# Blockwise attention and a tanh-shrink layer on one core: transposes one by one inside the units, small weight sums moved into two products, other accumulation banks

## The chip, the cores and the metric

One core of one Trainium2 chip runs the kernel. The metric is device time in microseconds (us) for one execution; lower is better. All work is in 32-bit floating point.

## The reference

`lam` decays the attention; the result is laid out token by token and goes through a dense layer, `h - tanh(h)`, and a second dense layer.

```python
# q, k, v: (4, 8, 768, 64); w_in: (512, 2048); w_out: (2048, 512)
for b in range(S // 64):
    qb, kb, vb = (t[:, :, 64*b : 64*b + 64] for t in (q, k, v))
    intra = einsum('bhic,bhjc->bhij', qb, kb) * Dmask          # lam**(i-j), i >= j
    out[:, :, sl] = einsum('bhij,bhjd->bhid', intra, vb) + einsum('bhid,bhde->bhie', qb * lam_pow, kv_state)
    kv_state = lam_block * kv_state + einsum('bhsd,bhse->bhde', kb * rev_pow, vb)
x = out.transpose(0, 2, 1, 3).reshape(3072, 512)
h = x @ w_in
result = (h - tanh(h)) @ w_out
```

## The kernel before

**Tiling.** The 3072 tokens are worked off in six groups (`g` = 0 to 5) of 512: 128 positions of each of the four batch entries, which the kernel calls blocks 0 to 3. Blocks 0 and 1 are the pair `P0`, 2 and 3 the pair `P1`. While the dense layers of group `g` run, the attention of group `h = g + 1` is slipped between them in small pieces: the function `pieces(g, place)` (L1157) looks up what is due at a named place.

**Dense layers.** Both are done by Strassen's scheme in its Winograd form: seven block products instead of eight, with sums before and after. The first layer is `up(g, u, n)` (L616) for four units `u` of 512 hidden columns and seven products `n`. Its results are the hidden quarters 11, 12, 21 and 22; `finish` (L638) takes each through tanh on ScalarE and a subtraction on VectorE (L641). In group 1 each unit runs the products in the order 2, 6, 5, 7, 1 (of the next unit), 4, 3. Products 6 and 7 share an accumulation bank, and ScalarE copies out the partial result of product 6 (L668) before product 7 may go on, and that of 7 (L670) before 4.

The second layer multiplies the hidden quarters by `w_out`. In group 1 its products P1 and P2 are plain (`down`, L845, matmul at L853) and P4, P5, P6, P7, P3 go one level deeper (`down_twice`, L899, matmuls at L918): seven small products x in the order 1, 2, 6, 5, 7, 3, 4, each 4 matmuls of 128x128. Its left sums s1 and s2 come from `sums_twice` (L878) on VectorE; small product 3 needs a further VectorE subtraction (the `hold` after x = 2, L923, shown as L876 in the trace, since the helper `hold` stands there). Group 2 (`GI`) is the first in which products 1 and 5 of the first layer go a level deeper too; their small weight sums are made once, in group 1, by `inner_weights` (L692): four VectorE subtractions of 128x128 per unit and per product (L699), then one DMA to the DRAM tensor `fine_in` (L700). Each such call takes a buffer of the tag `sums`, of which there are four; s1 and s2 of `sums_twice` take buffers of the same tag.

**Queues.** GpSimd (POOL) issues the DMAs that bring `w_out` factors into a ring of seven buffers `wb` (L799, L802, L805), the stores of results (L814) and the writes to `fine_in`, all in one queue in order. SyncE (SP) issues the loads of q, k and v; for groups 2 to 5 q and k come as `q_blk` and `k_blk` in a layout that lets VectorE turn 32x32 pieces (L361, `STREAM_TRANSPOSE`), 4 buffers for all.

**Order.** A scheduler places instructions on each engine by priority, unless they go through `tc.keep_in_program_order` (in the code also `tied(yes, ...)` and `hold`): such instructions of an engine keep the order of the program among themselves. An engine then works strictly in the order so fixed. PSUM accumulation banks are given out by tag: `att` has four, `ya`, `yb`, `z` and `w` one each; a bank can be given out again only when its last reader is done.

Of the kernel before, what the change touches and what calls it, by code (L numbers as in the profile page):

```python
# [9 lines left out]
F32 = mybir.dt.float32  # L10
# [14 lines left out]
def kernel(  # L25
# [324 lines left out]
    tr, sc, kdec, xt = {}, {}, {}, {}  # L350
    P0, P1 = (0, 1), (2, 3)

    def att_transpose(g, bs):
        for b in bs:
            load(g * B + b + 1)
            t = raw[g, b]
            qt = work.tile([128, NP, BLK], F32, name="qt", tag="qt")
            kt = work.tile([128, NP, BLK], F32, name="kt", tag="kt")
            for dst, x in ((qt, "q"), (kt, "k")):
                if g >= GB:  # L360
                    tc.keep_in_program_order(nc.vector.transpose(out=dst.rearrange("d p (t r) -> d p r t", r=4),  # L361
                                                                 in_=t[x + "b"].rearrange("d p (r a) -> d p r a", r=4)[:, :, :, 0:32]))
# [250 lines left out]
            hid[g, c] = gpool.tile([128, NU, 2, HB], F32, name=f"g{c}", tag=f"g{c}")  # L613
        return hid[g, c]

    def up(g, u, n, wait=False):  # L616
        a, bname = FACT[n]
        wt = {"A11": w1[u][:, 0:2, 0], "A12": w1[u][:, 2:4, 0], "S3": w1[u][:, 0:2, 1], "A22": w1[u][:, 2:4, 1],
              "S1": ws[u][:, 0], "S2": ws[u][:, 1], "S4": ws[u][:, 2]}[a]
        x = xt[g][bname] if bname != "B11" else xt[g, 0][:, 0:2]  # L620
        key = ("up", g, u)
        if g >= GI:
            if n in (2, 6):
                seeded(g, u, "w" if n == 2 else "y")
            if n == 6 and u:
                seeded(g, u, "z")
            t, first = banks["up", g, u, {2: "w", 3: "z"}.get(n, "y")].rearrange("q (m c) -> q m c", m=2), False
        else:
            t, first = product_bank(key, n)
        for m in range(2):  # L630
            for kt in range(2):
                tied(g == 0, nc.tensor.matmul(out=t[:, m, :], lhsT=wt[:, kt, ts(m, 128)], rhs=x[:, kt, :],  # L632
                                              start=first and m == 0 and kt == 0, stop=kt == 1, skip_group_check=True))

        def dst(c):
            return hidden(g, c)[:, u]

        def finish(c, src):  # L638
            th = work.tile([128, 2, HB], F32, name="th", tag="th")
            tied(g == 0, nc.scalar.activation(th, src, AF.Tanh))  # L640
            tied(g == 0, nc.vector.tensor_tensor(dst(c), src, th, op=AL.subtract))  # L641

        if g >= GI:
            if n == 2:
                finish(11, t)
            elif n == 6:
                nc.scalar.activation(dst(12), t, AF.Copy)
            elif n == 7:
                def end():
                    nc.vector.tensor_tensor(dst(22), dst(22), t, op=AL.add)  # L650
                    finish(22, dst(22))

                if wait:
                    return end
                end()
            elif n == 4:
                finish(21, t)
            else:
                nc.vector.tensor_tensor(dst(12), dst(12), t, op=AL.add)  # L659
                finish(12, dst(12))  # L660
            return
        y, z, w = (banks[key, x].rearrange("q (m c) -> q m c", m=2) if (key, x) in banks else None for x in "yzw")
        if n == 1:
            begin_second(key)
        elif n == 2:
            finish(11, w)
        elif n == 6:
            tied(g == 0, nc.scalar.activation(dst(12), y, AF.Copy))  # L668
        elif n == 7:
            tied(g == 0, nc.scalar.activation(dst(22), y, AF.Copy))  # L670
            tied(g == 0, nc.vector.tensor_tensor(dst(22), dst(22), z, op=AL.add))
            finish(22, dst(22))
        elif n == 4:
            finish(21, y)
        elif n == 3:
            tied(g == 0, nc.vector.tensor_tensor(dst(12), dst(12), z, op=AL.add))
            finish(12, dst(12))
            if g:
                up_sums(g, u)

    def up_sums(g, u):
        c11, c12, c22, s1 = (hidden(g, c)[:, u] for c in (11, 12, 22, "S1"))
        nc.vector.tensor_tensor(s1, c12, c22, op=AL.add)
        nc.vector.tensor_tensor(c12, c11, c12, op=AL.subtract)

    INNER = (1, 5)
    toks = {}
# [199 lines left out]
    def sum_third(g, n):  # L887
# [3 lines left out]

    PLACES = {GI - 1: {4: ("att", "yb"), 5: ("att", "w"), 6: ("yb", "z"), 7: ("w", "att"), 3: ("z", "att")},
              NG - 1: {4: ("att", "att"), 7: ("att", "yb"), 5: ("att", "w"), 2: ("yb", "ya"), 6: ("w", "att")}}
    PLACES.update({g: {4: ("att", "att"), 7: ("att", "yb"), 5: ("att", "w"), 1: ("yb", "z"), 2: ("w", "ya"),
                       6: ("z", "att"), 3: ("ya", "att")} for g in range(GI, NG - 1)})
# [1 line left out]
    def down_twice(g, n):  # L899
        a11, a12, a21, a22 = quarter(g, n)  # L900
        s1, s2 = low.pop((g, n))
        places = PLACES[g][n]
        begins = (1, 2) if places[0] == "att" else (2,)
# [79 lines left out]
    def up_plain(u, cs):  # L983

        hm = {}
        for c in cs:
            a, t = divmod(c - 11, 10)
            tag = ("ya", "yb" if u != 2 else "w", "z", "w")[2 * t + a]
            hm[c] = bank("h", tag, 1).rearrange("q (m c) -> q m c", m=2)
        for i in range(KI):  # L990
            for c in cs:
                a, t = divmod(c - 11, 10)
                for m in range(2):
                    tied(u == 0 or u == 2 and cs[0] == 11, nc.tensor.matmul(  # L994
                        out=hm[c][:, m, :], lhsT=w1[u][:, i, a, ts(m, 128)], rhs=xt[0, t][:, i, :],
                        start=m == 0 and i == 0, stop=i == KI - 1, skip_group_check=True))
                if (i, c) != (KI - 1, cs[-1]):
                    yield
        for c in cs:
            th = work.tile([128, 2, HB], F32, name="th", tag="th")  # L1000
            tied(True, nc.scalar.activation(th, hm[c], AF.Tanh))
            tied(True, nc.vector.tensor_tensor(hidden(0, c)[:, u], hm[c], th, op=AL.subtract))  # L1002
        yield
# [92 lines left out]
    weights(2 * KI + 1)  # L1096
    for n in (2, 6, 5, 7):
        up(0, 1, n)
        if n == 6:
            weights(2 * KI + 2)  # L1100
            load(B + 2)
# [55 lines left out]
    def pieces(g, at_):  # L1157
# [40 lines left out]
    def second_units(g):  # L1198
        for u in range(NU):
            for n in (2, 6, 5, 7, 1, 4, 3):  # L1200
                if n != 1:
                    up(g, u, n)
# [12 lines left out]
    def later_units(g):  # L1215
        made = [fine_factors(n) for n in (1, 2)] if g == GI else ()
        for u in range(NU):
            if made and u in (0, 2):
                next(made[u // 2])
            for n in ("next", 3, "S", 4) if u == 0 else (6, "next", 7, 3, "S", 4) if u + 1 < NU else (  # L1220
                    6, 3, 7, "S", "P4", "cover", 4):
                if n == "next":
                    up(g, u + 1, 2)
                elif n == "S":
                    up_sums(g, u)
                elif n == "P4":
# [4 lines left out]
                    else:  # L1231
                        every(down(g, 1))
                else:
                    up(g, u, n)
            pieces(g, u)
            if made and u in (0, 2):
                every(made[u // 2])

    def later_products(g):
        product = down_twice(g, 4)  # L1240
# [94 lines left out]
```

## Time and profile before

| | us |
|---|---|
| median of the three runs shown (655.16 to 657.22) | 656.59 |
| the profiled execution | 657.74 |
| its span, first to last instruction | 655.9 |
| idle time of TensorE in the span | 15.6 |
| VectorE busy / waiting for a tanh (L641) in all | 492.8 / 56.2 |

The span is what the profile sees of the profiled execution; 1.8 us lie around it. The clock granted to TensorE was 1.00 throughout. In the listings a line gives start, length (both us), engine, source line, operation and operands (output<-inputs); in brackets, the idle time before it and what ended that. A length includes the tail of a pipelined instruction, so that neighbours overlap; distances between starts are what counts.

### The profile page before, as it was taken

To read this page: it belongs to the slowest core of one execution; us is meant where nothing else is said; L and a number is where in the kernel's file an instruction comes from. 1 tells how busy PE (TensorE), PEld (TensorE's weight loads), DVE (VectorE), ACT (ScalarE), POOL (GpSimd) and SP (SyncE) were. 2 spreads that over 40 slices of the span, in tenths; PEclk is the share of its full clock that TensorE was granted. 3 is DMA by queue.
4 is the path that set the end of the run, shared out by engine and by line. 5 is a ranking of instruction groups with operands and counts; after the bars stand their busy time and mean duration, and the time that the engine had idled before them with its cause. 6 is when DMAs were issued, how large, how long until landed. Compare 5 with 4: busy or idle time off the path is not lost.

```text
span 655.9 us, 14773 instructions
## 1 busy us (share of the span) xinstructions
PE 640.3 (98%) x5792; PEld 589.3 (90%) x5792; DVE 492.8 (75%) x884; ACT 240.8 (37%) x484; POOL 231.0 (35%) x396
## 2 busy tenths in 40 slices
PE   7899999999999999999999999999999999999998
PEld 6688888888888999988899988999988999988997
DVE  4687997896976875889868768878768878356583
ACT  3687773513231223352122453222344212444110
POOL 2120246774113554342556100546202356300450
PEclk9999999999999999999999999999999999999999
DMA  9978978999358877999978765779672687610582
GB/s 214 216 200 207 237 231 287 332 319 313 104 156 201 260 241 238 247 270 255 295 235 302 196 141 135 233 238 303 208 155 80 212 287 246 210 45 0 157 284 74
DMA packets 108261, 140.45 MB, mean 214 GB/s; under 512 B 64032, under 2 KB 81568, under 8 KB 108192
## 3 DMA queue, kind: packets, MB, share of 16 engines
q0 software_dynamic: 29840, 97.54, 46.3%
q1 hardware_dynamic: 78208, 41.96, 27.6%
q8 instruction: 46, 0.75, 0.5%
q14 instruction: 23, 0.19, 0.1%
q10 hardware_dynamic: 144, 0.00, 0.0%
HBM read 117.18 MB, written 23.86 MB: 215 GB/s over the span
## 4 chain that ended last, share of the span: by engine, by line
PE 66%; DVE 6%; issue 5%; DMA 4%; POOL 3%; ACT 1%; POOLq 0%; DVEq 0%; ACTq 0%
PE y L918 14%; PE y L632 13%; PE zw L918 11%; PE z L632 4%; PE y L726 4%; PE w L632 4%; PE z L726 2%; PE acc L1024 2%; PE y L853 2%; DMA wb<-fine 2%; POOL wb L802 2%; DMA fine<-f 2%; PE sp L450 1%; PE op L500 1%; PE w L726 1%
## 5 line engine op out<-in xcount | busy, mean ns | idle before, releaser
L802 POOL DMA_DIRECT2D wb<-fine x217 | 117.1, 540 | 206.6 <-PE y L918 104.6
L918 PE MATMUL y<-wb,g 128*128 128x128 f32 x624 | 81.4, 276 | 1.9 <-DVE ss L457 0.9
L921 ACT ACTIVATE q<-y 128x128 f32<-128x128 f32 x108 | 30.0, 278 | 138.2 <-PE y L918 138.2
L918 PEld LDWEIGHTS y<-wb,g 128*128 128x128 f32 x624 | 75.3, 192 | 3.0 <-DVE ss L457 1.1
L918 PE MATMUL zw<-wb,g 128*128 128x128 f32 x416 | 55.1, 275 | 0.6 <-DMA wb<-fine 0.6
L918 PEld LDWEIGHTS zw<-wb,g 128*128 128x128 f32 x416 | 50.6, 192 | 1.0 <-PE y L918 0.6
L641 DVE TENSOR_TENSOR g<-g,th 128x512 f32<-128x512 f32 x42 | 29.1, 692 | 26.8 <-ACT th L640 26.7
L632 PE MATMUL y<-xt,w 128*128 128x256 f32 x200 | 47.0, 380 | 0.3 <-DVE g L1002 0.3
L640 ACT ACTIVATE th<-g 128x512 f32<-128x512 f32 x42 | 26.5, 630 | 54.8 <-DVE g L659 22.9
L994 PE MATMUL h<-xt,w 128*128 128x256 f32 x192 | 44.4, 383 | 2.1 <-DVE w L325 1.1
L632 PEld LDWEIGHTS y<-xt,w 128*128 128x128 f32 x200 | 37.5, 190 | 5.7 <-DVE g L1002 0.7
L994 PEld LDWEIGHTS h<-xt,w 128*128 128x128 f32 x192 | 35.6, 190 | 7.9 <-DVE g L1002 1.4
L632 PE MATMUL w<-xt,w 128*128 128x256 f32 x168 | 40.4, 382 | 0.0
L632 PE MATMUL z<-xt,ws 128*128 128x256 f32 x168 | 39.7, 379 | 0.0
L632 PE MATMUL y<-tt,w 128*128 128x256 f32 x160 | 38.1, 381 | 0.0
L632 PE MATMUL y<-tt,ws 128*128 128x256 f32 x160 | 38.1, 380 | 0.0
L632 PEld LDWEIGHTS z<-xt,ws 128*128 128x128 f32 x168 | 31.9, 190 | 4.3
L632 PEld LDWEIGHTS w<-xt,w 128*128 128x128 f32 x168 | 31.1, 190 | 4.3 <-ACT w L603 0.2
L632 PEld LDWEIGHTS y<-tt,w 128*128 128x128 f32 x160 | 30.2, 190 | 4.2
L632 PEld LDWEIGHTS y<-tt,ws 128*128 128x128 f32 x160 | 30.0, 190 | 3.9
L918 PE MATMUL y<-wb,s 128*128 128x128 f32 x248 | 32.8, 275 | 0.6 <-issue 0.6
L918 PE MATMUL zw<-wb,s 128*128 128x128 f32 x248 | 32.8, 275 | 0.0
(216 smaller groups left out, 1372.4 us busy)
## 6 DMA issues: line engine op xcount, KB each, us to landing
wb<-fine POOLq DMA_DIRECT2D x217, 256.0 KB, 3.7
fine<-f POOLq DMA_DIRECT2D x24, 256.0 KB, 5.0
wb<-fine_in POOLq DMA_DIRECT2D x24, 256.0 KB, 4.1
raw<-in_moe_w_out_dram POOLq DMA_DIRECT2D x10, 512.0 KB, 5.6
raw<-in_moe_w_in_dram SPq DMA_DIRECT2D x8, 512.0 KB, 5.2
raw<-in_moe_w_in_dram SPq DMA_DIRECT2D x16, 256.0 KB, 6.1
q_blk<-in_q_dram SPq DMA_DIRECT2D x32, 128.0 KB, 4.1
k_blk<-in_k_dram SPq DMA_DIRECT2D x32, 128.0 KB, 4.9
```

The lines of the kernel that those rows point to most:

```text
L450: tied(True, nc.tensor.matmul(out=dst, lhsT=keys(p, j, late_), rhs=qt[ts(j, 64), p, rows], start=True, stop=True))
L500: tied(True, nc.tensor.matmul(out=dst(n, p, j)[:, HF:BLK], lhsT=vn[:, 2 * p + j, :], rhs=ss[:, j, p % 2, 1 + p // 2, :], start=first and n ...
L632: tied(g == 0, nc.tensor.matmul(out=t[:, m, :], lhsT=wt[:, kt, ts(m, 128)], rhs=x[:, kt, :], start=first and m == 0 and kt == 0, stop=kt = ...
L640: tied(g == 0, nc.scalar.activation(th, src, AF.Tanh))
L641: tied(g == 0, nc.vector.tensor_tensor(dst(c), src, th, op=AL.subtract))
L726: tied(True, nc.tensor.matmul(out=dst[:, ts(u, 128)], lhsT=a, rhs=b, start=x in (1, 2, 5) and u == 0, stop=True, skip_group_check=True))
L802: nc.gpsimd.dma_start(out=t.rearrange("p m c -> p (m c)"), in_=fine[TWICE.index(n_), SLOT.index(x_)].rearrange("p u c -> p (u c)"))
L853: nc.tensor.matmul(out=t[:, m, :], lhsT=a[:, u, kt, ts(m, 128)], rhs=wb[:, kt, :], start=first and u == 0 and m == 0 and kt == 0, stop=u = ...
L918: tied(True, nc.tensor.matmul(out=dst, lhsT=a[:, u, :], rhs=wb[:, ts(u, 128)], start=x in begins and u == 0, stop=u == NU - 1, skip_group_ ...
L921: nc.scalar.activation(keep, dst, AF.Copy)
L994: tied(u == 0 or u == 2 and cs[0] == 11, nc.tensor.matmul(out=hm[c][:, m, :], lhsT=w1[u][:, i, a, ts(m, 128)], rhs=xt[0, t][:, i, :], star ...
L1024: nc.tensor.matmul(out=acc[n][:, r, :], lhsT=a[:, ts(r, 128)], rhs=b, start=kt == 0 and r == 0, stop=kt == KH - 1, skip_group_check=True)
```

## The change

1. **Transposes.** In group 1 (which prepares group 2) both transposes of a block used to be made together at the places 0, 2 and 3; now the eight single transposes (q and k of four blocks) stand one at each `finish` of quarter 22 or 12, between its tanh and its subtraction. From group 2 on the same holds for blocks 2 and 3, at (unit, quarter) = (0, 12), (1, 22), (1, 12), (2, 22). Blocks 0 and 1 stay where they were.
2. **VectorE order.** The subtractions, additions and `up_sums` of the units from group 1 on are tied to program order.
3. **Small weight sums.** `inner_weights` used to follow each unit of group 1. Now its four calls for product 1 stand between the steps of P1 and its four calls for product 5 between the steps of P2.
4. **Second set of finer factors** (`fine_factors`, group 2): loaded from unit 1 on, and its subtractions after product 7 of unit 2, not at the end of unit 2.
5. **Group 0.** `sums_first(0)` stands earlier, `sums_in(0)` after the qd products of the next piece; the banks of unit 3 (12 in `yb`, 22 in `z`) change.
6. **Bank of P4 in group 1:** `w` in place of `att`.

```diff
+    def turn_blocks(g, b, x):
+        if x == 0:
+            load(g * B + b + 1)
+            tr[g, b] = [work.tile([128, NP, BLK], F32, name=n, tag=n) for n in ("qt", "kt")] + [None]
+        turn_block(tr[g, b][x], raw[g, b]["qk"[x] + "b"])
...
         def finish(c, src):
             th = work.tile([128, 2, HB], F32, name="th", tag="th")
             tied(g == 0, nc.scalar.activation(th, src, AF.Tanh))
-            tied(g == 0, nc.vector.tensor_tensor(dst(c), src, th, op=AL.subtract))
+            if g:
+                pieces(g, ("t", u, c))
+            tied(g == 0 or inside, nc.vector.tensor_tensor(dst(c), src, th, op=AL.subtract))
...
-    PLACES = {GI - 1: {4: ("att", "yb"), 5: ("att", "w"), 6: ("yb", "z"), 7: ("w", "att"), 3: ("z", "att")},
+    PLACES = {GI - 1: {4: ("w", "yb"), 5: ("att", "w"), 6: ("yb", "z"), 7: ("w", "att"), 3: ("z", "att")},
...
-            tag = ("ya", "yb" if u != 2 else "w", "z", "w")[2 * t + a]
+            tag = ("ya", "yb", "z", "w")[2 * t + a]
+            if u == 2 and c == 21:
+                tag = "w"
+            elif u == NU - 1:
+                tag = {12: "yb", 22: "z"}.get(c, tag)
...
     for n in (2, 6, 5, 7):
         up(0, 1, n)
+        if n == 5:
+            sums_first(0)
...
-    sums_first(0)
     sums_first(1)
     load_weights(NU * KI)
     load(2 * B)
-    sums_in(0)
-    turns = [(2, (11, 21), 1, 1, (), ((att_transpose, 1, P0), (att_qd, 1, P0))),
+    turns = [(2, (11, 21), 1, 1, (), ((att_transpose, 1, P0), (att_qd, 1, P0), (sums_in, 0))),
...
         if g == 1:
-            table.update({0: [(att_transpose, h, P0)], 1: [(att_scores, h, P0), (att_qd, h, P0)]})
-        table.update({2 if g == 1 else 1: [(att_transpose, h, (2,))], 3 if g == 1 else 2: [(att_transpose, h, (3,))]})
+            table[1] = [(att_scores, h, P0), (att_qd, h, P0)]
+            turned = [(u, c) for u in range(NU) for c in (22, 12)]
+        else:
+            turned = [(0, 12), (1, 22), (1, 12), (2, 22)]
+        table.update({("t", u, c): [(turn_blocks, h, B - len(turned) // 2 + n // 2, n % 2)]
+                      for n, (u, c) in enumerate(turned)})
...
     def second_products(g):
         sums_twice(g, 4)
         sums_once(g, 11, "S1", 11)
-        every(down(g, 2))
+        product = down(g, 2)
+        for x in range(NU):
+            next(product)
+            inner_weights(x, INNER[1:])
         sums_twice(g, 5)
...
                     pieces(g, u)
-                    inner_weights(u, INNER[:1])
-                    every(down(g, 1))
+                    product = down(g, 1)
+                    for x in range(NU):
+                        inner_weights(x, INNER[:1])
+                        next(product)
...
-            inner_weights(u, INNER if u + 1 < NU else INNER[1:])
...
-            if made and u in (0, 2):
-                next(made[u // 2])
+            if made and u < 2:
+                next(made[u])
...
+                    if made and (u, n) == (2, 7):
+                        every(made[1])
```

More of the change, by code (lines that the diff above doesn't have):

```diff
@@ L351, with turn_block @@
     P0, P1 = (0, 1), (2, 3)
+    def turn_block(dst, x):
+        tc.keep_in_program_order(nc.vector.transpose(out=dst.rearrange("d p (t r) -> d p r t", r=4),
+                                                     in_=x.rearrange("d p (r a) -> d p r a", r=4)[:, :, :, 0:32]))
+    def turn_blocks(g, b, x):
[3 more added lines that the diff above has]
+        turn_block(tr[g, b][x], raw[g, b]["qk"[x] + "b"])
     def att_transpose(g, bs):
@@ L360, in att_transpose @@
                 if g >= GB:
-                    tc.keep_in_program_order(nc.vector.transpose(out=dst.rearrange("d p (t r) -> d p r t", r=4),
-                                                                 in_=t[x + "b"].rearrange("d p (r a) -> d p r a", r=4)[:, :, :, 0:32]))
+                    turn_block(dst, t[x + "b"])
                 else:
@@ L614, in hidden, with up @@
         return hid[g, c]
-    def up(g, u, n, wait=False):
+    def up(g, u, n, wait=False, inside=False):
         a, bname = FACT[n]
@@ L649, in end @@
                 def end():
-                    nc.vector.tensor_tensor(dst(22), dst(22), t, op=AL.add)
+                    tied(inside, nc.vector.tensor_tensor(dst(22), dst(22), t, op=AL.add))
                     finish(22, dst(22))
@@ L658, in up @@
             else:
-                nc.vector.tensor_tensor(dst(12), dst(12), t, op=AL.add)
+                tied(inside, nc.vector.tensor_tensor(dst(12), dst(12), t, op=AL.add))
                 finish(12, dst(12))
@@ L670, in up @@
             tied(g == 0, nc.scalar.activation(dst(22), y, AF.Copy))
-            tied(g == 0, nc.vector.tensor_tensor(dst(22), dst(22), z, op=AL.add))
+            tied(g == 0 or inside, nc.vector.tensor_tensor(dst(22), dst(22), z, op=AL.add))
             finish(22, dst(22))
@@ L675, in up @@
         elif n == 3:
-            tied(g == 0, nc.vector.tensor_tensor(dst(12), dst(12), z, op=AL.add))
+            tied(g == 0 or inside, nc.vector.tensor_tensor(dst(12), dst(12), z, op=AL.add))
             finish(12, dst(12))
@@ L682, in up_sums @@
         c11, c12, c22, s1 = (hidden(g, c)[:, u] for c in (11, 12, 22, "S1"))
-        nc.vector.tensor_tensor(s1, c12, c22, op=AL.add)
-        nc.vector.tensor_tensor(c12, c11, c12, op=AL.subtract)
+        tied(True, nc.vector.tensor_tensor(s1, c12, c22, op=AL.add))
+        tied(True, nc.vector.tensor_tensor(c12, c11, c12, op=AL.subtract))
     INNER = (1, 5)
@@ L902, in down_twice @@
         places = PLACES[g][n]
-        begins = (1, 2) if places[0] == "att" else (2,)
+        begins = (1, 2) if places[0] == "att" or (g, n) == (GI - 1, 4) else (2,)
         y, zw = (bank(name, t, 4 if t == "att" else 1) for name, t in zip(("y2", "zw"), places))
@@ L1201, in second_units @@
                 if n != 1:
-                    up(g, u, n)
+                    up(g, u, n, inside=True)
                 elif u + 1 < NU:
@@ L1222, in later_units @@
                 if n == "next":
-                    up(g, u + 1, 2)
+                    up(g, u + 1, 2, inside=True)
                 elif n == "S":
@@ L1233, in later_units @@
                 else:
-                    up(g, u, n)
+                    up(g, u, n, inside=True)
+                    if made and (u, n) == (2, 7):
+                        every(made[1])
             pieces(g, u)
-            if made and u in (0, 2):
-                every(made[u // 2])
+            if made and u == 0:
+                every(made[0])
     def later_products(g):
```

## The prediction

> **What bounds the kernel now.** First the page: the busy time of the engines, and the chain that ended last.
>
> ```profile
> span 655.9 us, 14773 instructions
> ...
> PE 640.3 (98%) x5792; PEld 589.3 (90%) x5792; DVE 492.8 (75%) x884; ACT 240.8 (37%) x484; POOL 231.0 (35%) x396
> ...
> PE 66%; DVE 6%; issue 5%; DMA 4%; POOL 3%; ACT 1%; POOLq 0%; DVEq 0%; ACTq 0%
> ```
>
> TensorE (PE) is busy for all but 15.6 us, and two thirds of the chain are PE. So a change pays only where it removes one of PE's few waits, and costs only where it makes one. Next, therefore, the waits in PE's timeline from the second group on and one ahead of it:
>
> ```profile
> 65.91 1.13 PE L994 MATMUL h<-xt,w 128*128 128x256 f32 x4 [0.99 <-DVE g L1002]
> ...
> 175.08 0.90 PE L450 MATMUL sp<-qt,kt 64*64 64x128 f32 x32 [0.22 <-DVE kt L361]
> ...
> 185.99 0.90 PE L450 MATMUL sp<-qt,kt 64*64 64x128 f32 x32 [0.32 <-DVE kt L361]
> ...
> 215.43 1.16 PE L918 MATMUL y<-wb,g 128*128 128x128 f32 x8 [0.69 <-ACT xt L404]
> ...
> 220.00 1.06 PE L918 MATMUL zw<-wb,g 128*128 128x128 f32 x8
> ...
> 307.50 1.13 PE L918 MATMUL y<-wb,s 128*128 128x128 f32 x8 [0.55 <-issue]
> ...
> 313.13 1.13 PE L918 MATMUL y<-wb,g 128*128 128x128 f32 x8 [0.93 <-DVE ss L457]
> 314.73 1.13 PE L918 MATMUL zw<-wb,g 128*128 128x128 f32 x8 [0.46 <-DMA wb<-fine]
> ```
>
> The row without brackets is small product 3 of P4: it starts 4.57 after P4. The seven waits are 4.2 us together: that is about all that better-placed VectorE work can win. Third, VectorE (DVE) and POOL where the sums move to:
>
> ```profile
> 202.92 0.69 DVE L641 TENSOR_TENSOR g<-y,th 128x512 f32<-128x512 f32 x1 [4.68 <-ACT th L640]
> ...
> 215.90 0.69 DVE L876 TENSOR_TENSOR s<-gS 128x512 f32<-128x512 f32 x1 [1.61 <-DMA fine_in<-ws]
> ...
> 217.84 0.68 DVE L876 TENSOR_TENSOR g<-g,s 128x512 f32<-128x512 f32 x1
> ...
> 225.35 0.69 DVE L876 TENSOR_TENSOR gS<-gS,s 128x512 f32<-128x512 f32 x1
> ```
>
> ```profile
> 209.93 1.53 POOL L700 DMA_DIRECT2D fine_in<-ws  x2
> 211.45 0.57 POOL L802 DMA_DIRECT2D wb<-fine  x1
> 213.01 0.71 POOL L814 DMA_DIRECT2D out_dram<-o  x1 [0.98 <-issue]
> 216.91 0.57 POOL L802 DMA_DIRECT2D wb<-fine  x1 [3.19 <-PE y L918]
> ```
>
> The 4.68 is idle time during P1, free to be filled. The 1.61 shows that s1 of P5 already waits for a `fine_in` write, as both use the four `sums` buffers: the writes were issued at 209.93 and 210.68 and VectorE went on at 215.90, 5.2 to 6.0 later. The DMA list has 2.9 as the median of the eight such writes and 2.5 as the shortest landing on that tensor. The 217.84 row is what small product 3 of P4 waits for, the 225.35 row the same for P5; between them VectorE never pauses for the profile.
>
> **The change part by part.** No instruction is added but for places in the order; the sum counts waits of PE. I use the instruction order of the two built programs, engine by engine, and the starts of before as the clock.
>
> *Group 0.* At 61.30 PE runs 16 matmul instructions of 0.216 and is through at 64.76; the 1.15 until 65.91 is a wait for VectorE, which did `sums_in(0)` (4 x 0.6 = 2.5) first. It now stands behind the qd products: VectorE is free 2.5 sooner, and no first matmul of the bank stands ahead of the attention any more. Gain 1.15, of which VectorE's rounding of weights later (PE waits of 0.53 and 0.40 for it at 118.94 and 131.70) may eat some; bounds 0 and -1.2, taken -1.0.
>
> *Units of group 1.* The transposes themselves (0.95 each, start to start) fall into waits for a tanh, and their blocks landed in time: the first is issued from 141.5 and due at 156. But PE's order changed with them. Before:
>
> ```profile
> 161.32 1.89 PE L632 MATMUL y<-tt,ws 128*128 128x256 f32 x8
> 163.05 1.89 PE L632 MATMUL z<-tt,ws 128*128 128x256 f32 x8
> 164.77 3.62 PE L632 MATMUL y<-xt,w 128*128 128x256 f32 x16
> ```
>
> The z row (product 5 of unit 1, 1.73) covers ScalarE's copy of product 6 (L668, 0.60 at 163.25). Now product 7 comes straight after 6, and 4 straight after 7, each behind a copy: 2 x about 0.75 (0.60 and a tenth each way). Product 1 of unit 2 then ends with nothing between it and product 2, which needs the copy at L603: 0.8. The scores of block 0 come late enough for their transpose, those of block 1 still wait, about 0.5, since VectorE runs behind the late tanh. 2 x 0.75 + 0.8 + 0.5 = 2.8, less the two waits removed (0.22 + 0.32 = 0.54): +2.2; I take 2.0. Bounds: 0 if covered after all, 3.0 if VectorE's lag grows. If it is later, P1 is later by as much.
>
> *P1.* Sixteen subtractions at 0.2 (start to start) are 3.2, inside the 4.68. Their four writes pass ahead of three `wb` loads of P4, due only at 215: nothing.
>
> *P2.* Here is the cost. VectorE meets the sixteen sums for product 5 after `sums_once`: with no eight sums and no k transpose (2.5) ahead of it that is at about 212.4, not 214.2. Two of the four `sums` buffers hold s1 and s2 of P4, so the four writes alternate on the other two, and s1, s2 of P5 use these again. The chain: sums of unit 0 (0.8, to 213.2); its write, which in POOL's queue now stands behind the store of P2's result (213.01 + 0.71): issued 213.6; landed 4.0 later, 217.6 (between 2.5 and 6.0); sums of unit 2 in the same buffer, 218.4; its write, landed 2.9 later, 221.3 (the DMA queues are nearly empty by then); s1, s2 and the subtraction in place, the second buffer being a write later, 221.3 + 0.7 + 0.2 + 1.3 = 223.5; then the `hold` for small product 3, which was at 217.84. It ends at 224.2, so product 3 starts 4.2 later than 220.00. VectorE is then the bound for one round more: from the 217.84 row to the end of the 225.35 row are 8.2, so product 3 of P5 can start at 223.5 + 8.2 = 231.7, where it started at 226.25: +5.5 in all. After P6 (`hold` 4.7 later, PE 6.25 later) PE leads again. Behind the stalled sums queue masks, qd and the sums of P5 to P7 on VectorE, and on POOL the loads for P5: free at 220, due at 226, landing in 3.7, so covered. Bounds: issue at 212.5 and 2.5 per landing give 221.4 for the end of the `hold`, and +2.7; 6.0 and 5 give +9.7. Both writes nearer the median: taken +5.5. The bank `w` lets P4 start 0.7 sooner, which is lost at product 3.
>
> *Group 2.* Earlier transposes and finer factors should free the three waits at 307 to 315 (1.94). Against it: product 7 of unit 3 follows 6 with no cover (0.75), and VectorE now stops inside unit 2 for the last factor load (issued 288.45, used from 298.78 before, now due at 293): some 1 to 2 us of lag that the masks hand on to P7. Bounds -1.2 and +1.5; taken 0.
>
> *Groups 3 to 5.* PE has no wait inside their units, and each `finish` is at most 0.3 later: 0, bounds -0.3 and +0.5.
>
> Sum: -1.0 + 2.0 + 5.5 + 0 = +6.5 on the span of 655.9, 662.4. The profiled execution (657.74) is 1.15 above the median shown; on the median, 656.6 + 6.5 = **663.1 us**.
>
> **The rivals.** *Quick writes.* Each landing takes 2.5, the shortest seen: P2 costs 2.7 and the sum is 3.7: 660.3. For it: queues are light after P2. Against: the two writes at 209.93 took over 5.
>
> *The clock falls.* The first 20 or so matmul instructions (128x128) come 0.213 apart, later ones 0.112: PE starts at half speed for some 4 us. If a stall of 4.2 brought that back, 4 us of work would cost 2 more; 1.25 of it lies under VectorE's bound at P5, so +0.8: 663.9. Against: the granted clock is 1.00 throughout, but no wait there exceeds 1.5. The Trainium skill (TensorE: Matmul & The Clock Gate, Part 1) says that after an idle window of about 3.4 us the clock drops to half, for about 3.4 us of work; the slow start agrees, no run here shows the drop.
>
> *Faster.* VectorE's 56.2 us of waiting for tanh absorb the transposes and every listed wait of PE goes, 4.2; unit 1 and the P2 chain cost nothing: 652.4. It holds if the `hold` of P4 ends by 219.1 (P4 from 214.7 plus 4.5). For it: 1.5 of slack today. Against: two landings in series from the end of P2 (210.8) leave 8.3 for a store, two issues, two landings of at least 2.5, and 3.6 of VectorE work, 10.8 together.
>
> *Moves cancel.* Quick writes with the unit's cost hidden and group 2 gaining: 2.7 - 1.0 - 1.2 = +0.5, 657.1.
>
> **How the numbers follow.** Forecast 0.60, quick writes 0.15, clock 0.10, faster 0.08, cancel 0.07. No change means within 0.3%, 2.0 us. Faster 0.09 (0.08 and 0.01 of the last), same 0.07 (0.06 of the last, 0.01 of the quick writes), slower 0.84. The range runs from below the quick writes to the long landings with part of the other upper bounds: 658.3 to 668.
>
> **What would show it.** In the profile after: a wait of VectorE for `fine_in` of 3 to 4 ahead of the third set of sums in P2 and of 2 to 3 ahead of s1 of P5; PE idle 4 to 5 ahead of small product 3 of P4, released by VectorE, and about 1 at that of P5; no wait at 66; three of 0.7 to 0.8 in unit 1 released by ScalarE; the waits near 313 present or not. It is wrong if VectorE passes P2 without waiting for `fine_in`, if PE reaches product 3 of P4 unhindered, or if P1's start (193.4) is not about 1 later.

## The result and the profile after

The changed kernel takes 665.19 us (median of 6 runs, 664.29 to 671.05), the kernel before 656.22 in the same comparison: 1.0157 times as long, interval 1.0117 to 1.0196. A second comparison gave 665.16 against 657.26: 1.0130 (1.0107 to 1.0153). The change makes the kernel slower, by 7.9 to 9.0 us. The profiled execution took 664.72; its span is 662.9 against 655.9.

First the page of the kernel after: the span, the engines, and the clock that TensorE was granted in 40 slices.

```profile
span 662.9 us, 14773 instructions
...
PE 643.3 (97%) x5792; PEld 590.8 (89%) x5792; DVE 495.1 (75%) x884; ACT 240.8 (36%) x484; POOL 231.5 (35%) x396
...
PEclk9999999999999799999999999999999999999999
```

There is as much work as before, yet PE is idle 4.0 us longer (19.6 against 15.6) and busy 3.0 us longer: the same matmuls ran slower for a while. The 7 in the clock row says where, in the slice from 215 to 232. In brackets is the idle time before a row; each row is a run of equal matmuls.

PE's timeline of the kernel after: the stretch that had the wait at 66, unit 1 of group 1, P4 and P5, and unit 3 of group 2.

```profile
60.30 3.62 PE L1010 MATMUL h<-xt,w 128*128 128x256 f32 x16
63.85 1.10 PE L496 MATMUL op<-qd,state 64*64 64x128 f32 x32
...
160.85 1.99 PE L642 MATMUL y<-xt,w 128*128 128x256 f32 x8 [0.69 <-ACT g L680]
163.54 1.99 PE L642 MATMUL y<-tt,w 128*128 128x256 f32 x8 [0.69 <-ACT g L682]
...
169.65 1.56 PE L642 MATMUL w<-xt,w 128*128 128x256 f32 x6 [0.67 <-ACT w L613]
...
217.88 1.06 PE L930 MATMUL y<-wb,g 128*128 128x128 f32 x8
224.76 2.08 PE L930 MATMUL zw<-wb,g 128*128 128x128 f32 x8 [5.82 <-DVE g L888]
226.63 1.92 PE L930 MATMUL y<-wb,g 128*128 128x128 f32 x8
228.33 1.78 PE L930 MATMUL y<-wb,gS 128*128 128x128 f32 x8
229.96 1.06 PE L930 MATMUL zw<-wb,gS 128*128 128x128 f32 x8
...
233.53 1.06 PE L930 MATMUL zw<-wb,gS 128*128 128x128 f32 x8
...
304.37 1.99 PE L642 MATMUL y<-xt,w 128*128 128x256 f32 x8 [0.75 <-ACT g L659]
306.65 1.99 PE L642 MATMUL z<-xt,ws 128*128 128x256 f32 x8 [0.28 <-ACT z L618]
```

The wait at 66 is gone. Unit 1 has three new waits for ScalarE's copies. Product 3 of P4 (224.76) waits 5.82 for VectorE, and the three groups behind the wait start 1.87, 1.70 and 1.63 apart where others start 0.89 apart, 2.5 more in all. In group 2 the 0.75 and 0.28 in unit 3 are new, the waits at 307.5, 313.1 and 314.7 of before are gone.

Why VectorE is late: its timeline in the kernel after, and then POOL's.

```profile
202.45 0.69 DVE L653 TENSOR_TENSOR g<-y,th 128x512 f32<-128x512 f32 x1 [2.73 <-ACT th L650]
...
216.72 0.29 DVE L711 TENSOR_TENSOR ws<-ws 128x128 f32<-128x128 f32 x1 [3.47 <-DMA fine_in<-ws]
...
220.55 0.69 DVE L888 TENSOR_TENSOR s<-gS 128x512 f32<-128x512 f32 x1 [1.88 <-DMA fine_in<-ws]
222.81 0.69 DVE L888 TENSOR_TENSOR s<-s,gS 128x512 f32<-128x512 f32 x1 [1.57 <-DMA fine_in<-ws]
...
224.02 0.68 DVE L888 TENSOR_TENSOR g<-g,s 128x512 f32<-128x512 f32 x1
...
231.54 0.68 DVE L888 TENSOR_TENSOR gS<-gS,s 128x512 f32<-128x512 f32 x1
```

```profile
211.33 0.72 POOL L826 DMA_DIRECT2D out_dram<-o  x1
212.61 0.78 POOL L712 DMA_DIRECT2D fine_in<-ws  x1 [0.56 <-DVE ws L711]
213.55 0.76 POOL L712 DMA_DIRECT2D fine_in<-ws  x1 [0.16 <-issue]
218.04 0.76 POOL L712 DMA_DIRECT2D fine_in<-ws  x1 [3.73 <-DVE ws L711]
220.17 0.76 POOL L712 DMA_DIRECT2D fine_in<-ws  x1 [1.37 <-issue]
```

The third set of sums in P2 waits 3.47 for a write of the first (issued 212.61), s1 of P5 for the write issued at 218.04, s2 for the one issued at 220.17. Only then come the subtraction and the `hold` of P4 (224.02), which frees PE at 224.76. The `hold` of P5 (231.54) is 7.52 behind it.

To sum up where the time went, the span is cut at three starts of the same PE work: the first matmul of unit 0 of group 1, that of P1, and small product 3 of P5. The table holds all profiled executions; differences of the first two columns are what the change did, as far as a stretch repeats.

| stretch, us | before | after | after again | experiments |
|---|---|---|---|---|
| A: start to units of group 1 | 145.61 | 142.57 | 142.91 | e1 143.02, e2 146.75, e3 143.87, e4 147.33, e5 145.38, e6 143.78, e7 145.62, e8 145.71, e10 147.22, e11 143.41, e12 144.41 |
| B: units of group 1 | 47.79 | 50.36 | 50.36 | e1 52.03, e2 50.36, e3 52.58, e4 50.35, e5 47.79, e6 47.77, e7 50.35, e8 47.78, e10 47.78, e11 47.78, e12 47.78 |
| C: P1 to product 3 of P5 | 32.85 | 40.60 | 40.92 | e1 32.10, e2 34.72, e3 40.87, e4 39.47, e5 46.96, e6 32.86, e7 41.38, e8 32.10, e10 40.96, e11 32.58, e12 32.10 |
| D: the rest | 429.70 | 429.39 | 427.84 | 428.2 to 431.9 |

A -3.04, B +2.57, C +7.75, D -0.31: together +6.97, the difference of the spans. B and C repeat to a few tenths from execution to execution; A and D do not, and A has a reason that is found below.

### The profile page after: what moved, and what is told of

Its sections match the earlier page's. It is cut to its first block, busy times and chain, and to the rows that moved or that the text cites. A ratio compares the mean times of both kernels' runs of the same rounds, so it can differ in the third digit from the quotient of the medians.

```text
span 662.9 us, 14773 instructions
## 1 busy us (share of the span) xinstructions
PE 643.3 (97%) x5792; PEld 590.8 (89%) x5792; DVE 495.1 (75%) x884; ACT 240.8 (36%) x484; POOL 231.5 (35%) x396
## 4 chain that ended last, share of the span: by engine, by line
PE 59%; issue 12%; DMA 5%; POOL 4%; DVE 3%; ACT 1%; POOLq 0%; DVEq 0%; ACTq 0%
PE y L930 14%; PE y L642 11%; PE zw L930 11%; PE z L642 4%; PE y L738 4%; PE w L642 4%; DMA fine<-f 2%; POOL wb L814 2%; PE acc L1040 2%; PE z L738 2%; PE y L865 2%; PE end L989 1%; DMA f<-factors 1%; PE w L738 1%; PE op L510 1%
```

## The experiments

Each was timed against the kernel before on one chip (medians of before 657.26 to 657.71 there). e1 to e4 ran together, then e5 to e8, then e9 to e12.

**e1: all small sums back in the units; e2: another buffer.**

```diff
 # e1: second_products and second_units as before
-            product = down(g, 2)
-            for x in range(NU):
-                next(product)
-                inner_weights(x, INNER[1:])
+            every(down(g, 2))
...
+            inner_weights(u, INNER if u + 1 < NU else INNER[1:])
 # e2: inner_weights
-            t = late["pool"].tile([128, 4, 128], F32, name="ws2", tag="sums", bufs=4)
+            t = (opool.tile([128, 4, 128], F32, name="ws2", tag="o") if n == 5 and u > 1 else
+                 late["pool"].tile([128, 4, 128], F32, name="ws2", tag="sums", bufs=4))
```

> All the small weight sums stand again at the ends of the units of group 1, as in the kernel before; the rest of the change stays. Theory (the loss is made in P2, where the sums for product 5 and s1, s2 of P5 share the sums buffers with writes to fine_in under way): the wait of 5.82 ahead of small product 3 of P4 is gone, the granted clock stays at 1.00, product 3 of P5 starts near 226 instead of 233.5, and the execution takes about 656.5 (655.5 to 658). Rival (the new order inside the units of group 1 costs as much): above 660, with the waits of unit 1 still at 2.0 together and product 3 of P5 at 228 or later.

> The sums stay where the change put them, in P1 and P2, but units 2 and 3 of product 5 write into two idle output buffers instead of the two sums buffers that units 0 and 1 use: only the reuse of a buffer behind a write is taken away. Theory: VectorE does the sixteen sums without a pause, s1 waits for the first write alone (until about 216.7), the hold of P4 ends near 219.3 and product 3 of P4 starts near 219.5, that of P5 near 227; no drop of the clock; the execution takes about 658 (657 to 660.5). Rival (the place of the sums, 16 subtractions of 0.2 ahead of P4's and P5's work on VectorE, is what costs): product 3 of P4 still after 222 and the time above 661.

e1: 660.25 (658.26 to 665.41), ratio 1.0056 (1.0032 to 1.0080). Stretch C falls to 32.10, which is 0.75 less than before: the stall is gone altogether, and bank `w` lets P4 start 0.7 sooner. So the theory holds for P2, and the time is still above its range and where the rival had it, as the units became longer, 52.03. Two waits in PE's timeline of e1 that the kernel after doesn't have, or has shorter:

```profile
172.28 1.99 PE L642 MATMUL z<-xt,ws 128*128 128x256 f32 x8 [0.61 <-DVE g L683]
...
176.85 0.90 PE L460 MATMUL sp<-qt,kt 64*64 64x128 f32 x32 [1.12 <-DVE kt L354]
```

With sums and single transposes both in the units, and VectorE's order fixed, VectorE falls behind there.

e2: 661.08 (658.31 to 664.99), 1.0059 (1.0036 to 1.0082); C is 34.72. VectorE and PE of e2:

```profile
221.63 0.69 DVE L889 TENSOR_TENSOR s<-gS 128x512 f32<-128x512 f32 x1 [2.34 <-DMA fine_in<-ws]
```

```profile
224.31 1.16 PE L931 MATMUL zw<-wb,g 128*128 128x128 f32 x8 [1.19 <-DVE g L889]
...
231.83 1.16 PE L931 MATMUL zw<-wb,gS 128*128 128x128 f32 x8 [1.00 <-DVE gS L889]
```

The sixteen sums run without a pause, one wait for a write is left, and PE's wait falls from 5.82 to 1.19, while the sums stay where the change put them. Of the 7.75 that C grew by, 5.9 (40.60 - 34.72) come with the reuse of two buffers behind writes under way. In the 1.9 that are left s1 still waits 2.34 for a write, since the sums of units 0 and 1 keep two of the `sums` buffers; how much is due to that and how much to the sums' place on VectorE, this run does not separate. The time is 0.6 above the theory's range, and product 3 of P4 starts behind the rival's 222, but this execution came late to P1 (A 146.75, see e6): counted from P1's start product 3 comes after 27.20, against 31.83 in the kernel after and 26.60 in the kernel before.

**e3: the matmuls tied to their written order.**

```diff
-                tied(g == 0, nc.tensor.matmul(out=t[:, m, :], lhsT=wt[:, kt, ts(m, 128)], rhs=x[:, kt, :],
+                tied(g < 2, nc.tensor.matmul(out=t[:, m, :], lhsT=wt[:, kt, ts(m, 128)], rhs=x[:, kt, :],
```

> The matmuls of group 1's units are kept in the order in which they are written, so that product 5 of unit 1 stands again between 6 and 7, and 1 of unit 2 ahead of 4. Theory (the three waits for ScalarE's copies in unit 1, 0.69, 0.69 and 0.67, are a cost of PE's order alone): they go, P1 starts about 2.0 sooner (near 190.9), the chain in P2 moves with it, and the execution takes about 662.7. Rival (VectorE's pace behind the late tanh sets P1, and the waits move to another place): P1 within 0.5 of 192.9, time 664 to 665.

670.89 (668.33 to 673.55), 1.0209 (1.0177 to 1.0240): the theory failed, and the rival was too mild. The three waits in unit 1 go, but the written order also puts the scores of blocks 0 and 1 ahead of product 2 of unit 2, where block 1's transpose is not ready. PE's timeline of e3, and its busy times and clock around it (PEclk is the number ahead of the DMA share):

```profile
174.83 0.90 PE L460 MATMUL sp<-qt,kt 64*64 64x128 f32 x32 [2.66 <-DVE kt L354]
```

```profile
172.00:175.00 3.00, 0.34 (x17) 0.20 (x13) 3.00 (x6) 0.63 (x1) 0.00 (x0) 1.00 0.44 112
175.00:180.00 5.00, 5.00 (x44) 4.12 (x41) 2.62 (x5) 0.56 (x1) 0.00 (x0) 0.66 0.67 158
```

A wait of 2.66 was enough to bring the clock to 0.66 in the next 5 us.

**e4: PE kept busy in its stall.**

```diff
+            if (g, n, x) == (1, 4, 3):
+                for _ in range(20):
+                    tied(True, nc.tensor.matmul(out=zw[:, 128:256], lhsT=zero["t"][:, 0:128], rhs=a11[:, 1, :],
+                                                start=False, stop=True, skip_group_check=True))
             wb = piece(g, n, x).rearrange("p m c -> p (m c)")
```

> Twenty matmuls more (4.5 at 0.223 each) on a block of zeros, added to the region of small product 3 of P4 just ahead of it, where PE waits 5.82: the result does not change, the stall of VectorE stays, PE only idles 1.4 instead of 5.8. One memset of 128x128 more on VectorE. Theory (the idle stretch brings the clock down): the granted clock stays at 1.00, the groups after 224.8 are 0.9 apart instead of 1.9, 1.7 and 1.6, VectorE's hold of P5 (done at 232.2) becomes the bound, product 3 of P5 starts near 232.3 instead of 233.5, and the execution takes about 1.2 less: 663.5. Rival (the slow groups come from something else, loads of wb or VectorE): they stay 1.6 to 1.9 apart, 664.7 or more.

667.59 (664.60 to 669.66), 1.0148 (1.0116 to 1.0181). The total missed its 663.5 and cannot show 1.2 us, as A was 147.33 in the profiled execution (why, see e6). The stretch itself does; PE's timeline of e4:

```profile
223.53 4.63 PE L930 MATMUL zw<-g,zero 128*128 128x128 f32 x40
229.63 1.16 PE L934 MATMUL zw<-wb,g 128*128 128x128 f32 x8 [1.47 <-DVE g L888]
230.62 1.06 PE L934 MATMUL y<-wb,g 128*128 128x128 f32 x8
231.52 1.06 PE L934 MATMUL y<-wb,gS 128*128 128x128 f32 x8
...
237.15 1.16 PE L934 MATMUL zw<-wb,gS 128*128 128x128 f32 x8 [1.00 <-DVE gS L888]
```

P4 to its product 3 is as long as ever (10.67 against 10.55), but the groups behind it are 0.99, 0.90 and 0.89 apart, and from there to product 3 of P5 are 7.52, set by VectorE, instead of 8.77. So the slow groups are the idle stretch's doing, and they cost 1.25.

**e5: the small sums alone, on the kernel before.** The edit is that of e1 the other way round.

> The kernel before with one part of the change alone: the small weight sums go from the units into P1 and P2; no transposes, no other order, no other bank. Theory (P2 makes the loss by itself): the units of group 1 are not longer than the 47.8 of before, as VectorE has less to do in them; P4 to its product 3 takes about 10.5 instead of 4.57, from there to product 3 of P5 about 8.8 instead of 6.25, with the clock down again; the execution takes about 665 (663 to 666.5). Rival (the loss needs the transposes inside the units, which make VectorE late for P2): P4 to product 3 under 7 and the time below 661.

669.24 (666.40 to 673.74), 1.0173 (1.0141 to 1.0206). The loss needs no transposes, as the theory has it, and is larger than it said; the units are 47.79, as before. VectorE and PE of e5:

```profile
208.18 0.27 DVE L699 TENSOR_TENSOR ws<-w 128x128 f32<-128x128 f32 x1
```

```profile
230.88 2.07 PE L918 MATMUL zw<-wb,g 128*128 128x128 f32 x8 [10.73 <-DVE g L876]
```

Here the sums for product 1 do not fall into P1's gap, where the kernel after has them from 195.92 on, but come behind its end, at 208.18. Their four writes then hold all four buffers when s1 of P4 wants one (VectorE waits 3.73, until 215.71), the sums for product 5 begin only at 219.92, and PE waits 10.73. The rest of the change roughly halves the damage (C 40.60 against 46.96). Fixing VectorE's order in the units is not what does it: in e10, which leaves it free there, the sums for product 1 start at 197.82, inside P1, and C is 40.96. In e5 these sums stand behind block 3's k transpose (207.24), in the kernel after ahead of it (204.09); no run moves that transpose alone.

**e6: group 0 alone; e7 and e8: its load first.** e6 is the kernel before with the first edit and the change's tags in `up_plain`. e7 is the kernel after with the second edit, e8 is e6 with the second edit and bank `w`.

```diff
 # e6, e8
+        if n == 5:
+            sums_first(0)
...
-    sums_first(0)
     sums_first(1)
...
-    sums_in(0)
-    turns = [(2, (11, 21), 1, 1, (), ((att_transpose, 1, P0), (att_qd, 1, P0))),
+    turns = [(2, (11, 21), 1, 1, (), ((att_transpose, 1, P0), (att_qd, 1, P0), (sums_in, 0))),
 # e7, e8
-                for names in ("qk", "v") if b == 2 else ("qkv",):
-                    for x in both:
-                        raw.setdefault((g, x), {})
+                for x in both:
+                    raw.setdefault((g, x), {})
+                for x, names in ((3, "k"), (2, "qk"), (3, "q"), (2, "v"), (3, "v")) if (g, b) == (1, 2) else [
+                        (x, names) for names in (("qk", "v") if b == 2 else ("qkv",)) for x in both]:
                         load_natural(g, x, names)
```

> The kernel before with the change to group 0 alone: the sums of unit 0 earlier, the sums of products 2 and 6 of the weights behind the qd products, the other banks there. Theory: the wait at 66 goes and PE reaches the transposes of block 3 about 2.2 sooner (74.1 instead of 76.4), but the load of that block's k (landed at 75.5 in the kernel before, at 74.6 to 77.5 in the runs with the change) is then the bound in some executions: the units of group 1 start 3.0 sooner where it is in time and up to 1.5 later where it lands at 77.5 and the clock falls; median about 656.5, range 654 to 660. Rival (the part gains its 3.0 always): median 654.7, range below 657. Rival (it gains nothing): 657.7.

> The kernel after, with the load of block 3's k (group 1) issued ahead of block 2's q and k and block 3's q, while SP waits for a buffer for that q. Theory (the spread of the kernel after, 664.3 to 671.1, and its late start of the units in some executions come from this one load): no wait for k ahead of the transposes at 74, the units of group 1 start near 142.5, and the executions lie between 663.5 and 666, median 664.6. Rival (the loads only swap places, and q of block 3 or k of block 2 is late instead): a wait of 1 or more at 70 or 74 for one of these, and the same spread up to 669.

> The kernel before with the parts of the change that gain, and only these: group 0 as changed, bank w for the first small product of P4, and block 3's k loaded first as in the run with that load alone; units, P1 and P2 as before. Theory: the units of group 1 start 3.0 sooner, P4 0.7 sooner, and nothing else moves: about 654 (653 to 655.5), faster than both kernels. Rival (later loads or VectorE take the gain back, as P4's product 3 is bound by its hold): 656 to 658.

e6: 657.32 (654.39 to 661.13), ratio 0.9996 (0.9971 to 1.0020): no change on average, between 1.9 faster and 1.3 slower by the interval; its executions lie within 6.7, those of the kernel before beside them within 6.5. In its profile PE comes to block 3's transposes at 74.82, 1.55 sooner than before, and waits 0.23 for k. How much it waits there differs from execution to execution. Of the eight profiles that have the change's group 0 and these loads and transposes as it has them (after twice, e1, e2, e3, e4, e6, e10) five show 0 to 0.69 and three 2.57 to 2.84. The worst case is seen in e10's timeline of PE, with its clock row for 78 to 82:

```profile
74.57 0.38 PE L376 MATMUL tp<-ident,k_nat 128*128 128x128 f32 x2
77.58 0.41 PE L376 MATMUL tp<-ident,k_nat 128*128 128x128 f32 x2 [2.63 <-DMA k_nat<-in_k_dram]
77.83 5.31 PE L1010 MATMUL h<-xt,w 128*128 128x256 f32 x16
```

```profile
78.00:82.00 4.00, 4.00 (x12) 3.21 (x12) 1.88 (x4) 2.44 (x4) 1.04 (x2) 0.57 0.21 60
```

Behind the wait the clock is 0.57, and sixteen matmuls that take 3.62 elsewhere take 5.31. That is why A is 142.6 to 143.9 in five of these profiles and 146.8 to 147.3 in three.

e7: 668.29 (667.08 to 671.01), 1.0176 (1.0146 to 1.0206); e8: 656.94 (652.76 to 661.16), 1.0004 (0.9975 to 1.0033). Both miss, much as the rivals said: the loads swap places. PE's timeline of e7:

```profile
71.12 0.41 PE L377 MATMUL tp<-ident,k_nat 128*128 128x128 f32 x2 [0.58 <-DMA k_nat<-in_k_dram]
...
73.20 0.41 PE L377 MATMUL tp<-ident,k_nat 128*128 128x128 f32 x2 [0.80 <-DMA k_nat<-in_k_dram]
...
77.18 0.63 PE L377 MATMUL tp<-ident,q_nat 128*128 128x128 f32 x4 [0.98 <-DMA q_nat<-in_q_dram]
```

Now block 2's k is late twice, and block 3's q. The loads as a whole come late for the faster group 0, and this other order is no cure.

**e9: the kernel after again; e10: VectorE not fixed in the units.**

```diff
                 if n != 1:
-                    up(g, u, n, inside=True)
+                    up(g, u, n)
...
-        tied(True, nc.vector.tensor_tensor(s1, c12, c22, op=AL.add))
-        tied(True, nc.vector.tensor_tensor(c12, c11, c12, op=AL.subtract))
+        tied(g >= GI, nc.vector.tensor_tensor(s1, c12, c22, op=AL.add))
+        tied(g >= GI, nc.vector.tensor_tensor(c12, c11, c12, op=AL.subtract))
```

> The kernel after, unchanged, a second time, on the same chip as the three next to it. Theory: P4 to its product 3 about 10.6 and from there to product 3 of P5 about 8.8, as the first time; the start of the units of group 1 moves with the load of block 3's k (wait at 74 between 0 and 2.9): 142.5 to 147.3; the execution takes 664 to 670.

> The kernel after, but VectorE's tanh sums and additions inside the units of group 1 are not fixed in their order; the single transposes stay where they are, and so do the sums in P1 and P2. In the built program PE's order in unit 1 is then that of before again (product 5 between 6 and 7, 1 of unit 2 ahead of 4), but the scores of block 0 stand later than in the run that tied the matmuls. Theory (the three waits for ScalarE's copies follow from fixing VectorE, as that moves PE's order): they go without a new wait for the scores, the units of group 1 take about 48.2 instead of 50.4, the chain in P2 stays, and the time is about 2 below that of the unchanged kernel after beside it. Rival (the transposes inside the units are what lengthens them): units of 50 or more, no gain.

e9: 665.16 (663.84 to 666.32), stretches A to C within 0.4 of the first time, D 1.6 shorter. e10: 666.48 (663.75 to 670.44), 1.0148 (1.0114 to 1.0183). Its units take 47.78, as long as before, with the single transposes in them, and PE's order in unit 1 is the old one:

```profile
162.92 1.89 PE L642 MATMUL y<-tt,ws 128*128 128x256 f32 x8
164.65 1.89 PE L642 MATMUL z<-tt,ws 128*128 128x256 f32 x8
166.38 3.62 PE L642 MATMUL y<-xt,w 128*128 128x256 f32 x16
```

Product 5 stands again behind 6 and covers its copy; none of these rows waits. So the 2.57 of stretch B come from fixing VectorE's order together with the transposes, which moves PE's order; the transposes as such cost nothing there. The total did not gain its 2: A was 147.22 in the profile, with a k wait of 2.63 in it.

**e11 and e12: what remains when the losses are taken out.** Both move block 3's transposes three steps later on PE; e11 is else e6 with bank `w`, e12 is the kernel after with e10's edit and product 5's sums at the units' ends.

```diff
-            steps(turn, KI - 2 * (turn is half))
+            steps(turn, KI + 3 * (u == 3) - 2 * (turn is half))
 # e12 also, in second_products and second_units
-            product = down(g, 2)
-            for x in range(NU):
-                next(product)
-                inner_weights(x, INNER[1:])
+            every(down(g, 2))
...
+            inner_weights(u, INNER[1:])
```

> The kernel before with the change's group 0 and its bank for the first small product of P4, and the transposes of block 3 moved three steps (2.6) later on PE, so that PE comes to them at 76.7 and not at 74.1. Units, P1 and P2 as before. Theory (the gain of 3.0 in group 0 is lost to the load of block 3's k, which lands at 74.5 to 77.5): waits of at most 0.8 there, no drop of the clock, units of group 1 from 142.7 to 143.5, P4 0.7 sooner; about 654 (652.5 to 655.5) against 657.4 of before, and a smaller spread. Rival (block 3's scores, or VectorE, are late in their turn): units from 144.5 or later, 656 to 658.

> The kernel after with three edits: VectorE not fixed in the units of group 1 (as in the run with that alone), product 5's sums back at the ends of the units and only product 1's in P1, block 3's transposes three steps later. Theory (with the chain of P2, the copies' waits and the k load gone, the rest of the change gains): units of group 1 from 143, 48 to 49 long, P4 to its product 3 4.6, and about 655 (653 to 657) in all. Rival (sums and transposes together overload VectorE in the units, as in the run with all sums back, units 52.0): 657 to 660.

e11: 656.24 (654.29 to 662.23), ratio 0.9999 (0.9976 to 1.0022). The k load no longer shows, and A is 143.41 as expected, but D is 431.93, with four waits of PE in group 2 between 305 and 315, 2.8 together, three of them for `wb` loads; the gain is lost there in the profiled execution. None of these waits is longer than 1.25, yet the clock falls behind them (0.53 from 316 to 318), and groups start 1.71 apart. PE's timeline of e11:

```profile
312.69 1.13 PE L918 MATMUL zw<-wb,g 128*128 128x128 f32 x8 [1.25 <-DMA wb<-fine]
314.30 1.92 PE L918 MATMUL y<-wb,s 128*128 128x128 f32 x8 [0.49 <-DMA wb<-fine]
316.01 1.91 PE L918 MATMUL zw<-wb,s 128*128 128x128 f32 x8
```

e12: 654.67 (654.11 to 656.37), 0.9964 (0.9945 to 0.9982): faster than the kernel before, and 10.5 below the kernel after (665.16 beside it). PE's timeline of e12:

```profile
77.01 0.60 PE L376 MATMUL tp<-ident,q_nat 128*128 128x128 f32 x4
77.44 0.83 PE L376 MATMUL tp<-ident,k_nat 128*128 128x128 f32 x4
...
217.15 1.06 PE L930 MATMUL y<-wb,g 128*128 128x128 f32 x8
218.04 1.06 PE L930 MATMUL zw<-wb,g 128*128 128x128 f32 x8
```

Hardly a wait for k (its row takes 0.83 where 0.60 is usual), none at product 3 of P4, units of 47.78, and no `wb` wait in group 2 (two waits for ScalarE, 0.75 and 1.26, stay in unit 3 there). e12 keeps the earlier factors and e11 has not; but e6, without them too, has no `wb` wait there, so that they are the reason is not shown. All twelve executions lie within 2.3 us, those of the kernel before beside them within 7.7.

## Why the prediction was right, and where its sizes were off

- *What bounds the kernel.* The forecast counted waits of PE alone. They are the larger part: of the 6.97, 4.0 are more idle time of PE. The other 3.0 are PE busy for longer, 2.5 of them the three slow groups behind the wait.
- *P2, +5.5.* The mechanism is as told: reuse of the `sums` buffers behind writes, a late `hold`, then one round of VectorE to P5. e1 and e2 show it from two sides. C grew by 7.75. Two sizes were off. "The second buffer being a write later" was taken as 0.9 after the first; POOL stood idle 1.37 between the two issues for nothing that the profile shows, and s2 started 2.26 after s1 (220.55 to 222.81). And the clock did fall: that was a rival with a price of 0.8; e4 puts it at 1.25. Counted from P1's start, s1 came 0.3 sooner than told, the `hold` of P4 1.0 later and product 3 of P5 2.3 later. The round of 8.2 from the `hold` of P4 to the end of P5's came out as told (224.02 to 232.22); but no wait of 1 at P5 followed, since PE itself was slow and came later than that. A slip without effect: 214.2 less 2.5 is 211.7, not 212.4, and VectorE met the sums at 211.30. From their own terms the two bounds come out some 0.2 lower.
- *Units of group 1, +2.0.* 2.57, with the waits named (0.69, 0.69, 0.67, and 0.33 for the scores). That they follow from PE's moved order is shown by e10. e3 shows that tying PE is not the cure: the next thing late is the scores.
- *Group 0, -1.0.* The step that was incomplete. The profile has -3.04: 1.00 is a difference in the first 38 us, ahead of the first edit; 1.26 is the wait at 66; the rest is less waiting for weights at 119 and 132, which the prediction had expected to grow. What it did not price is the load of block 3's k, landed at 75.47 in the trace of before and due at 76.8 there: a margin of 1.3 that a gain of 2 uses up. Late, it takes back up to 2.8 and the clock 1.1 to 1.7 more. On average (e6) no gain of this part shows.
- *P1, nothing.* P1 to P2 is 10.36 in both.
- *Group 2, 0.* The units of group 2 to the inner product of group 3 take 193.20 before and 193.15 after: three waits of 1.94 gone, 0.75 comes, as named, and 0.28 at the next product.
- *The condition on P1's start.* The text held it against itself if P1 did not start about 1 later. It started 0.47 sooner, since group 0 gained 2 more than priced in that execution; the units' cost in it is right.

So the sign was right by the mechanism, but that the span's +6.97 lies so near the +6.5 is in part luck: group 0 came out 2.0 below its term in that execution, the units and P2 together 2.8 above theirs. On the medians the change costs 7.9 to 9.0, while B and C alone add up to 10.3; the difference is no larger than what e6's interval leaves open for group 0 together with the spread of D. The rivals "quick writes", "faster" and "moves cancel" are out; "the clock falls" came true on top of the forecast.

What stays open: the 1.37 of POOL, what makes e5's loss in P2 so much larger than the change's, and whether the `wb` waits of e11 in group 2 come in most of its executions. That all of product 5's writes get buffers of their own in P2 was tried with two of four only, and not in the units of e12.

## What to carry to other kernels

Work that fits an idle stretch of its engine still has to be followed to the buffers it holds and to the queue that empties them: here sixteen operations of 0.2 us made a stall of 5.8, because their buffers were the next operands' buffers. A gain ahead of a load uses up that load's margin, so look at landing times against due times before it is counted, and expect a spread, not a shift, where the two meet. Fixing one engine's order lets a scheduler move another's: compare the order of all engines.

## What the runs showed of the hardware

The granted clock of TensorE fell to 0.50 behind single waits of 2.57 us (e2), 2.63 (e10), 2.66 (e3) and 2.84 (e4), and within those of 5.82 (the kernel after) and 10.73 (e5). The length of one wait does not decide it: in e11 the clock fell at 314.45 behind waits of 0.50, 1.25 and 0.49 close together, in e5 at 329.14 behind 0.60 and 1.21, and in e8 a wait of 1.80 left it at 1.00.

The half clock lasted 3.41 us behind the short waits, 6.82 in the kernel after and 13.65 in e5, and the two stretches of e10 start 146.78 apart, 43 times 3.413: the clock seems to be set in fixed steps of 3.41. Counted in such steps, from the first rise of the clock on, PE was busy for 0 to 1.67 us in the step ahead of each drop (0.78 in e10 from 74.73, 1.45 in e2, 1.60 in e5 ahead of 329.14, 1.67 in e11), and for 1.61 (e8, from 69.49) or more in every step at full clock that no drop followed, in all fourteen profiles. So what counts in these profiles is how much of a step PE is idle, about half, and several short waits add up.

The Trainium skill (TensorE: Matmul & The Clock Gate, Part 1) puts the drop after an idle window of about 3.4 us, with a window that runs free of the kernel; the runs agree on a clock of about half (groups 1.87 apart for 0.89) and on the 3.4 us, and differ in that the window need not be idle throughout. Its advice against idle gaps of PE agrees with e4: twenty matmuls on zeros kept the clock at 1.00 and saved 1.25 us in that stretch.
